# Order of the loads, shared Q/K buffers and new places for batches 1 to 3 in a fused window-attention and mixer kernel

## The chip, the core and the metric

The kernel runs on one core of one Trainium2 chip. The metric is the device time of a run in microseconds (us), given as the median of 11 runs. A core has five engines that each work through a queue of their own in order: TensorE (PE; its weight loads are shown apart as PEld), VectorE (DVE), ScalarE (ACT), GpSimd (POOL) and SyncE (SP). They wait for one another through semaphores. Transfers between HBM and SBUF are issued from a queue (here POOL's for loads with a change of type, SP's for stores and for transposes inside SBUF) and carried out by 16 DMA engines. Matmuls write to PSUM, of which VectorE and ScalarE copy the results out.

## The reference

```python
# attention, 8 batches, 8 heads, 576 rows, head size 64, window 64
scores = scale * np.matmul(q, k.transpose(0, 1, 3, 2))
mask = (rel >= 0) & (rel < window)            # rel = row - column
attn = exp(where(mask, scores, -1e9) - max) ; attn = attn / (sum + 1e-09)
x = (attn @ v), heads side by side            # [8, 576, 512]
# mixer
h = xt @ U @ V          # over the 576 rows, rank 32; xt is x transposed
u = x + h.transpose(0, 2, 1)
ch = np.maximum(u @ w_ch1, 0.0) @ w_ch2       # 512 -> 2048 -> 512
out = u + ch
```

Each row sees at most 64 columns, so only the diagonal and the next lower block of 64 by 64 are computed.

## The kernel before, in words

**Two streams woven together.** The mixer works on 9 chunks of 512 rows (all 8 x 576 = 4608 rows laid end to end). Chunk c has 32 slots: 16 pieces `ch1` (four matmuls of 512 columns each, then a ReLU out of PSUM on ScalarE or VectorE, by the table `DVE_RELU`), and 16 pieces `ch2` (four output tiles of 128 rows, four quarters each; after the fourth quarter VectorE adds u and SP stores the tile). Behind each slot stand pieces of the attention of batch b = c + 1, as the tables `PLACE`, `PLACE_1` and `PLACE_2` say: a piece's number is the slot behind which it is written. This written order is each engine's queue. There is no planner: the order is by hand. Batch 0's attention runs ahead of the chunks, with idle matmuls (`turn_over`, L718) in between.

**The pieces of a batch.** `T` brings Q and K into transposed form: for batches 0 and 1 from a grouped load (six rows per partition) by TensorE transposes (`tr`, L262) with a copy by ScalarE (K) and VectorE (Q), for the later ones by `TX`, ten DMA transposes from SP's queue (L285) into `kf` and `qf`, of which there is one each. `S` is the scores of two heads and their exponential (L326, L346), the last piece, `SC8`, those of the last block of all heads; `M` multiplies with the mask on VectorE. `PV` multiplies with V (L388) and normalises on VectorE with a reciprocal and a multiplication (L410, L411). V is kept twice: `vA` by tiles of 128 rows, and `vB` shifted by 64 rows, which is copied out of `vA` (`shift_v`, L149 and L152): on POOL for batches 0 and 1, on VectorE for the others, in slot 8 or 24. `U` is the low-rank product with its copy `hh` (L502), `V` its second half (`psv`, L566) with the addition to x (L579), and `UT` the transposed u that `ch1` reads: for batches 0 to 2 by TensorE (L598) through the single buffer `tp` and a ScalarE copy (L601), from batch 3 on (`NXU` = 3) by DMA transposes from SP's queue (L594).

**The loads.** POOL issues them in this order: Q and K of batch 0, V of batch 0, the first weights `w1b` (L217), Q and K of batch 1 in grouped form (L117), V of batch 1 (L135, L140), the second weights `w2b` in four parts (L225), then Q and K of batch 2, V of batch 2 and so on. Each DMA of POOL's queue waits for the one eight places before it to land: the first `w2b` load is the eighth after the second `w1b` load, and was issued as that landed.

Of the kernel before, what the change touches and what calls it, by code (L numbers as in the profile page):

```python
# [8 lines left out]
ACT = mybir.ActivationFunctionType  # L9
# [7 lines left out]
def kernel(  # L17
# [24 lines left out]
    NGR = 2  # L42
    NXB = 2
    NXU = 3
    GP = S // GR
    NFULL = S // P
    CH = 512
# [9 lines left out]
    outf = out.rearrange("b s m -> (b s) m")  # L57

    const = ctx.enter_context(tc.tile_pool(name="const", bufs=1))
    kg_pool = ctx.enter_context(tc.tile_pool(name="kg", bufs=4))  # L60
    uT_pool = ctx.enter_context(tc.tile_pool(name="uT", bufs=3))
    u_pool = ctx.enter_context(tc.tile_pool(name="un", bufs=14))
    c1_pool = ctx.enter_context(tc.tile_pool(name="c1", bufs=1))
# [24 lines left out]
    xs = [const.tile([P, NT, H, D], BF16, name=f"xs{i}") for i in range(2)]  # L88
    vA = [const.tile([P, NFULL, H, VW], BF16, name=f"vA{i}") for i in range(2)]
    vB = [const.tile([P, NFULL, H, VW], BF16, name=f"vB{i}") for i in range(2)]  # L90
    kn = [const.tile([P, NT, H, D], BF16, name=f"kn{i}") for i in range(2)]
    qn = [const.tile([P, NT, H, D], BF16, name=f"qn{i}") for i in range(2)]

    kf = const.tile([P, NT * HP * P], BF16, name="kf")
    qf = const.tile([P, NT * HP * P], BF16, name="qf")
    kt, qt = ([f[:, j * S : (j + 1) * S] for j in range(HP)] for f in (kf, qf))
    kx, qx = (f.rearrange("p (t j w) -> p t j w", t=NT, j=HP) for f in (kf, qf))
    pts = const.tile([P, HP, 2, NB - 1, W], BF16, name="pts")
    ptl = const.tile([P, HP, 2, W], BF16, name="ptl")

# [3 lines left out]
    def load_kq(b, split):  # L104
        grouped = b < NGR
        if grouped:
            kb = kg_pool.tile([GP, H, GR, D], BF16, name="kg")
            qb = kg_pool.tile([GP, H, GR, D], BF16, name="qg")
        else:
            kb, qb = kn[b % 2], qn[b % 2]  # L110
        loaded[b] = (kb, qb)
        if grouped:
            step = 4 if split else H
            for h0 in range(0, H, step):
                hs = slice(h0, h0 + step)
                for t, src in ((kb, k), (qb, q)):
                    nc.gpsimd.dma_start(  # L117
                        out=t[:, hs, :, :].rearrange("p h c d -> p h (c d)"),
                        in_=src[b, hs, :, :].rearrange("h (p c) d -> p h (c d)", c=GR),
                    )  # L120
                    yield
        else:
            for t in range(NT):
                rows = P if t < NFULL else W
                for dst, src in ((kb, k), (qb, q)):
                    nc.gpsimd.dma_start(  # L126
                        out=dst[0:rows, t, :, :],
                        in_=src[b, :, t * P : t * P + rows, :].rearrange("h p d -> p h d"),
                    )
                yield  # L130
# [15 lines left out]
    def shift_v(b, copy, tiles):  # L146
        va, vb = vA[b % 2], vB[b % 2]
        lo, hi = tiles.start, tiles.stop
        copy(out=vb[W:P, lo:hi, :, :], in_=va[W:P, lo:hi, :, :])  # L149
        last = min(hi, NFULL - 1)  # L150
        if lo < last:
            copy(out=vb[0:W, lo:last, :, :], in_=va[0:W, lo + 1 : last + 1, :, :])  # L152


    kq0 = load_kq(0, True)
# [35 lines left out]
    nc.vector.memset(xs[0][W:P, NT - 1, :, :], 0.0)  # L191
    nc.vector.memset(xs[1][0:W, 0, :, :], 0.0)
    for i in range(2):
        nc.vector.memset(kn[i][W:P, NFULL, :, :], 0.0)
        nc.vector.memset(qn[i][W:P, NFULL, :, :], 0.0)


    nc.sync.dma_start(
# [16 lines left out]
    w1v = moe_w_ch1.rearrange("(c p) n -> p c n", p=P)  # L215
    for lo, hi in ((0, 1024), (1024, 2048)):
        nc.gpsimd.dma_start(out=w1b[:, :, lo:hi], in_=w1v[:, :, lo:hi])  # L217
    for t in range(NFULL):
        shift_v(0, nc.gpsimd.tensor_copy, range(t, t + 1))
    for _ in load_kq(1, False):  # L220
        pass
    load_v(1)
    w2v = moe_w_ch2.rearrange("(i p) m -> p i m", p=P)
    for i in range(0, NFC, 4):
        nc.gpsimd.dma_start(out=w2b[:, i : i + 4, :], in_=w2v[:, i : i + 4, :])  # L225
    for t in range(NFULL):
        shift_v(1, nc.gpsimd.tensor_copy, range(t, t + 1))

    u_tiles = {}
    uT_tiles = {}  # L230
# [7 lines left out]
    def attention(b, spare=False):  # L238
# [4 lines left out]
        x = xs[odd]  # L243
        g0 = (b * S) // P
        pcs = {}

        grouped = b < NGR
        turn = [0]
# [26 lines left out]

        def TQ(j):
            def f():
                copy = nc.scalar.copy if spare and j == 3 else nc.vector.tensor_copy
                copy(out=place_of(qt, j), in_=tr(qb, j, b == 1))
            return f  # L280

        def TX(t):
# [306 lines left out]
        def UT(t):  # L589
            def f():  # L590
                g = g0 + t
                dst = uT_of(g // TPC)[:, g % TPC, :, :]
                if b >= NXU:
                    nc.sync.dma_start_transpose(out=dst, in_=u_tiles[g][:])  # L594
                    return
                tp = ps_tp.tile([P, NDC, P], BF16, name="tpu", tag="tp")
                for dc in range(NDC):
                    nc.tensor.transpose(  # L598
                        tp[:, dc, :], u_tiles[g][:, dc * P : (dc + 1) * P], ident[:]
                    )  # L600
                nc.scalar.copy(out=dst, in_=tp[:])  # L601
            return f
# [26 lines left out]
        return pcs  # L629


    DVE_RELU = {0: (8, 10, 11, 13, 15), 1: (2, 4, 6, 9, 10, 12, 13)}
    DVE_RELU_N = (0, 1, 2, 4, 5, 6, 8)

    def mlp(c):
        uTc = uT_of(c)
        c1 = [None] * NFC

        def ch1(i):
            def f():  # L640
                ps = psum["mm"].tile([P, CH], FP32, name="psA", tag="mm")
                for dc in range(NDC):
                    nc.tensor.matmul(  # L643
                        ps[:],
                        w1b[:, dc, i * P : (i + 1) * P],
                        uTc[:, :, dc, :],
                        start=(dc == 0),
                        stop=(dc == NDC - 1),
                    )
                c1[i] = c1_pool.tile([P, CH], BF16, name=f"c1_{i}")  # L650
                if i in DVE_RELU.get(c, DVE_RELU_N):
                    nc.vector.tensor_relu(out=c1[i][:], in_=ps[:])  # L652
                else:
                    nc.scalar.activation(out=c1[i][:], in_=ps[:], func=ACT.Relu)  # L654
            return f

        acc = {}
# [19 lines left out]
                    nc.sync.dma_start(out=outf[g * P : (g + 1) * P, :], in_=osb[:])  # L677
            return f

        return [ch1(i) for i in range(NFC)] + [ch2(t, r) for t in range(TPC) for r in range(4)]  # L680


    PLACE = {
# [7 lines left out]
    }  # L691
    PLACE_0 = {"V": [0, 0, 1, 2, 2, 3, 4, 4]}
    PLACE_1 = {
        "T": [11, 11, 12, 12, 13, 13, 14, 14],
        "S": [12, 13, 14, 15, 15],
        "M": [13, 14, 15, 16, 16],
        "PV": [17, 17, 18, 19, 20],
        "U": [22],
        "V": [23, 24, 25],
        "UT": [25, 26, 27, 28, 29],  # L700
        "TX": [20, 22, 24, 26, 28],
    }
    PLACE_2 = {
        "S": [8, 8, 11, 11, 13],
        "M": [9, 10, 12, 13, 14],
        "PV": [16, 16, 18, 18, 20],
        "TX": [13, 14, 15, 16, 17],
        "U": [21],
        "V": [23, 24, 25],
        "UT": [25, 26, 27, 28, 29],  # L710
    }


# [2 lines left out]
    def turn_over(n, cols=CH):  # L716
# [14 lines left out]
        op0=ALU.mult,  # L731
        op1=ALU.add,
    )
    pair = maskA[:, 0, 1:3, :].rearrange("p (o n) w -> p o (n w)", o=1)
    nc.vector.tensor_copy(
        out=maskA[:, 0, 3:7, :].rearrange("p (o n) w -> p o (n w)", o=2),
        in_=pair.to_broadcast([P, 2, 2 * W]),
    )
    nc.vector.tensor_copy(out=maskA[:, 0, 7, :], in_=maskA[:, 0, 1, :])
    nc.vector.tensor_scalar(  # L740
        out=maskB[:],
        in0=maskA[:, 0, :, :],
        scalar1=30000.0,
        scalar2=-30000.0,
        op0=ALU.mult,
        op1=ALU.add,
    )
    order = "K0 K1 B0 B1 Q0 Q1 S0 S1 K2 K3 B2 Q2 B3 Q3 S2 S3 B4 S4"
    for what in order.split():
        j = int(what[1])  # L750
        if what[0] in "SB":
            a[what[0]][j]()
        else:
            a["T"][2 * j + (what[0] == "Q")]()
        if what == "Q1":
            load_low_rank()
        turn_over({"B1": 1, "Q1": 1, "S1": 1, "Q3": 1}.get(what, 0))
    nc.vector.tensor_copy(out=maskA[:, 1, :, :], in_=maskA[:, 0, :, :])
    nc.scalar.copy(out=ub[0][:], in_=uf[0][:])
    nc.scalar.copy(out=vrep[:, W : W + S], in_=vf[:])  # L760
    for t in range(NT + 2):
        if t < NT:
# [5 lines left out]
            a["idle"](1)  # L768
    for f in [a["U"][NT - 1]] + a["X3"] + a["HT"]:
        f()  # L770
    first.close()
    psum["mm"] = ctx.enter_context(
        tc.tile_pool(name="ps_mm", bufs=3, space=bass.MemoryType.PSUM)
    )


    for c in range(NCH):
        slots = [[] for _ in range(NSLOT + 1)]

        def place(b, parts, where):  # L780
            if b not in att:
                att[b] = attention(b)
            for part in parts:
                for f, s in zip(att[b][part], where[part]):
                    slots[s].append(f)

        b = c + 1
        if b < B:
# [3 lines left out]
            if b + 1 < B:  # L792
                load_v(b + 1)
            if b + 2 < B:
                for _ in load_kq(b + 2, False):
                    pass
            where = {1: PLACE_1, 2: PLACE_2}.get(b, PLACE)
            if b < NXB:
                place(b, ("T",), where)
            if b == 1:  # L800
# [2 lines left out]
            for bs, slot in ((b, 8), (b + 1, 24)):  # L803
                if 1 < bs < B and (slot == 24) == (bs > 2):
                    slots[slot].append(
                        lambda bs=bs: shift_v(bs, nc.vector.tensor_copy, range(NFULL))
                    )
            place(b, ("S", "M", "PV"), where)
            if NXB <= b + 1 < B:
                place(b + 1, ("T",), {"T": where["TX"]})  # L810
# [35 lines left out]
```

The softmax here doesn't subtract the row's maximum and nothing guards it: scores larger than these inputs give would overflow.

## Time and profile before

| | us |
|---|---|
| median of 11 runs | 321.82 |
| lowest and highest of them | 320.56 and 324.8 |
| the profiled execution's own time | 321.33 |
| its span | 319.6 |
| first product of chunk 0 | 23.66 |
| first `ch2` of chunk 0 | 43.29 |
| first product of chunk 1 | 65.97 |
| first product of chunk 2 | 99.77 |
| first product of chunk 3 | 132.08 |
| last store issued | 316.63 |

How to read the lines: a row of groups gives line, engine, operation, the tiles it writes and reads, shapes and count, then busy time and the mean of one in ns, and the idle time ahead of it with what ended it. A row of the timeline gives start, length, engine, line, operation and tiles; matmuls overlap, so the next one starts before the length of the last has run out. A row of waits gives who waited for whom, the sum, the count and the longest. The granted clock is a share of TensorE's full speed.

### The profile page before, as it was taken

The page shows a single profiled execution, that of the slowest core. Times are in us where ns is not written, and L with a number is a line of the kernel's source. Part 1 is how long each engine was busy: PE and PEld are TensorE (multiplying, and loading weights), DVE is VectorE, ACT ScalarE, POOL GpSimd, SP SyncE. Part 2 cuts the span into 40 slices and gives each one's busy share as a digit, 9 for nine tenths or more (in the row PEclk, how much of TensorE's full clock was granted, in tenths as well). Part 3 has the DMA queues.
Part 4 walks back from the last instruction along what each step waited for, and adds up shares of the span by engine and source line. Part 5 has one row for each costly group of instructions (what it writes and reads, how often), then busy time and mean ns, then how long its engine had stood idle before and what let it go on. Part 6 is the DMA issues. An engine that isn't in the chain of part 4 may idle for free.

```text
span 319.6 us, 6811 instructions
## 1 busy us (share of the span) xinstructions
PE 306.4 (96%) x2829; PEld 149.8 (47%) x2855; DVE 162.8 (51%) x293; ACT 101.8 (32%) x160; POOL 103.2 (32%) x134
## 2 busy tenths in 40 slices
PE   7779988999999999999999999999999999999995
PEld 6544543544545544454445444544454444444442
DVE  4464584527775745475647464756374443016011
ACT  3545550336224450335024502450245003201500
POOL 8692696645734744554541400000000000000000
PEclk9999997999999999999999999999999999999999
DMA  7999999999999999999999982344200520020011
GB/s 105 161 223 202 156 200 171 120 167 191 143 138 210 161 139 149 184 193 157 138 210 177 144 158 100 68 100 95 105 2 2 115 99 2 9 89 33 2 66 66
DMA packets 151871, 39.56 MB, mean 124 GB/s; under 512 B 140960, under 2 KB 146080, under 8 KB 151840
## 3 DMA queue, kind: packets, MB, share of 16 engines
q0 software_dynamic: 100096, 18.36, 78.7%
q1 hardware_dynamic: 51744, 20.77, 35.8%
q8 instruction: 22, 0.36, 0.4%
q14 instruction: 9, 0.07, 0.1%
HBM read 37.14 MB, written 9.44 MB: 146 GB/s over the span
## 4 chain that ended last, share of the span: by engine, by line
PE 79%; DMA 13%; POOL 5%; issue 1%; SPq 1%; DVE 0%; POOLq 0%
PE psA L643 35%; PE psU L665 35%; DMA qg<-in_q_dram 5%; DMA vA<-in_v_dram 3%; DMA qn<-in_q_dram 2%; DMA uTc<-un 2%; PE psv L566 2%; PE sc L326 2%; PE xw L388 2%; POOL vB L149 1%; PE xr L388 1%; POOL vB L152 1%; PE pshh L487 1%; POOL vA L135 1%; PE tpu L598 1%
## 5 line engine op out<-in xcount | busy, mean ns | idle before, releaser
L665 PE MATMUL psU<-w2b,c 128*128 128x512 bf16 x555 | 131.5, 382 | 3.6 <-DMA w2b<-in_moe_w_ch_dram 2.2
L643 PE MATMUL psA<-uTc,w1b 128*128 128x512 bf16 x576 | 131.0, 380 | 0.5 <-DVE uTc L553 0.4
L665 PEld LDWEIGHTS <-c 128*128 128x128 bf16 x576 | 55.5, 98 | 67.2 <-issue 3.8
L643 PEld LDWEIGHTS <-w1b 128*128 128x128 bf16 x576 | 54.0, 98 | 65.1 <-issue 1.3
L654 ACT ACTIVATE c<-psA 128x512 bf16<-128x512 f32 x83 | 49.6, 597 | 91.2 <-PE psA L643 91.2
L674 DVE TENSOR_TENSOR osb<-psU,un 128x512 f32<-128x512 f32 x36 | 24.9, 691 | 84.3 <-PE psU L665 84.0
L652 DVE TENSOR_SCALAR c<-psA 128x512 bf16<-128x512 f32 x61 | 42.0, 689 | 24.7 <-PE psA L643 24.7
L579 DVE TENSOR_TENSOR un<-psv,xs 128x512 bf16<-128x512 f32 (+1 forms) x40 | 25.4, 684 | 22.1 <-PE psv L566 22.0
L135 POOL DMA_DIRECT2D vA<-in_v_dram x32 | 28.2, 888 | 22.6 <-DVE rce L444 7.8
L346 ACT ACTIVATE pts<-sc 128x1024 bf16<-128x1024 f32 x32 | 31.4, 1028 | 2.7 <-PE sc L326 2.6
L126 POOL DMA_DIRECT2D qn<-in_q_dram x30 | 25.7, 855 | 19.1 <-DMA qn<-in_q_dram 7.8
L126 POOL DMA_DIRECT2D kn<-in_k_dram x30 | 25.4, 848 | 18.8 <-DMA vA<-in_v_dram 9.5
L379 ACT ACTIVATE ptl<-low 128x256 bf16<-128x256 f32 x5 | 1.9, 384 | 64.8 <-PE high L326 64.8
L352 DVE TENSOR_TENSOR pts<-pts,maskA 128x1024 bf16<-128x1024 bf16 x28 | 19.2, 686 | 0.1
L326 PEld LDWEIGHTS <-kf 64*64 64x64 bf16 x704 | 10.0, 107 | 8.5 <-issue 8.3
L326 PE MATMUL sc<-qf,kf 64*64 64x128 bf16 (+1 forms) x624 | 12.2, 212 | 1.6 <-issue 0.8
L388 PEld LDWEIGHTS <-pts 128*64 128x64 bf16 x512 | 10.4, 112 | 6.8 <-issue 4.6
L566 PE MATMUL psv<-hh,vrep 128*128 128x512 bf16 x40 | 12.5, 379 | 0.0
L455 DVE TENSOR_TENSOR xs<-xw,rcw 128x896 bf16<-128x896 f32 x10 | 10.9, 1092 | 0.3
L411 DVE TENSOR_TENSOR xs<-xr,rcp 128x512 bf16<-128x512 f32 (+1 forms) x15 | 10.4, 691 | 0.5
L502 ACT CAST hh<-pshh 128x512 bf16<-128x512 f32 x7 | 4.1, 581 | 18.4 <-PE pshh L495 18.4
L601 ACT COPY uTc<-tpu 128x512 bf16<-128x512 bf16 x9 | 5.3, 586 | 11.2 <-PE tpu L598 11.2
(102 smaller groups left out, 160.2 us busy)
## 6 DMA issues: line engine op xcount, KB each, us to landing
out_dram<-osb SPq DMA_DIRECT2D x36, 256.0 KB, 2.4
vA<-in_v_dram POOLq DMA_DIRECT2D x32, 128.0 KB, 10.3
kn<-in_k_dram POOLq DMA_DIRECT2D x24, 128.0 KB, 12.3
qn<-in_q_dram POOLq DMA_DIRECT2D x24, 128.0 KB, 12.0
w1b<-in_moe_w_ch_dram POOLq DMA_DIRECT2D x2, 1024.0 KB, 15.8
w2b<-in_moe_w_ch_dram POOLq DMA_DIRECT2D x4, 512.0 KB, 13.1
kg<-in_k_dram POOLq DMA_DIRECT2D x2, 288.0 KB, 5.8
qg<-in_q_dram POOLq DMA_DIRECT2D x2, 288.0 KB, 6.8
```

What stands on the lines that cost most here:

```text
L126: nc.gpsimd.dma_start(out=dst[0:rows, t, :, :], in_=src[b, :, t * P : t * P + rows, :].rearrange("h p d -> p h d"),)
L135: nc.gpsimd.dma_start(out=va[:, t, :, 0:D], in_=v[b, :, t * P : (t + 1) * P, :].rearrange("h p d -> p h d"),)
L326: nc.tensor.matmul(sc[g][r0 : r0 + W, col * W : (col + n) * W], keys_of(j, u, rs), queries_of(j, blk, n, rs), start=not spare, stop=last o ...
L346: nc.scalar.activation(out=dst, in_=sc[:], func=ACT.Exp, scale=scale)
L352: nc.vector.tensor_tensor(out=dst, in0=dst, in1=maskA.rearrange("p g n w -> p g (n w)"), op=ALU.mult)
L388: nc.tensor.matmul(dst, pts[:, h // 2, h % 2, blk, :] if blk < NB - 1 else ptl[:, h // 2, h % 2, :], rhs, start=True, stop=True,)
L579: nc.vector.tensor_tensor(out=u_tiles[g][rs, :], in0=ps[0][rs, n, :], in1=x[rs, t, :, :].rearrange("p h d -> p (h d)"), op=ALU.add,)
L643: nc.tensor.matmul(ps[:], w1b[:, dc, i * P : (i + 1) * P], uTc[:, :, dc, :], start=(dc == 0), stop=(dc == NDC - 1),)
L652: nc.vector.tensor_relu(out=c1[i][:], in_=ps[:])
L654: nc.scalar.activation(out=c1[i][:], in_=ps[:], func=ACT.Relu)
L665: nc.tensor.matmul(acc[t][:], c1[i][:, t * P : (t + 1) * P], w2b[:, i, :], start=(i == 0), stop=(i == NFC - 1),)
L674: nc.vector.tensor_tensor(out=osb[:], in0=acc[t][:], in1=u_tiles[g][:], op=ALU.add)
```

## The change

- **Order of the loads.** The four `w2b` loads are issued ahead of the five loads of batch 1's V.
- **Copies of V.** For batch 0 five of the seven copies stay on POOL and two go to ScalarE. For batch 1 all seven leave POOL for VectorE, as pieces `SV` in slots 21 to 24, each written ahead of the `PV` of the same slot.
- **Buffers.** `kf` and `qf` exist twice, by the batch's parity. The grouped loads no longer have buffers of their own: they use the memory of `kn` and `qn`. So batch 3's Q and K loads are written behind slot 14 of chunk 0.
- **Places.** Batches 1, 2 and 3 have new tables. A number above 100 means the next chunk. Batch 1's PV goes from slots 17 to 20 to slots 21 to 24, and what follows it moves accordingly; batch 2's scores go from slots 8 to 13 to slots 14 to 18; batch 3 gets a table of its own.
- **Transposes of u.** Batch 3's go from SP's DMA to TensorE (`NXT` = 4), while the other choices that hung on `NXU` stay.
- **Mask.** The bias mask is made of three blocks and repeated on ScalarE with one block on VectorE; the multiplied mask is completed only after batch 0's attention.
- **Others.** The first two `ch1` pieces of chunk 0 are joined, with their matmuls in turn; the ReLU tables change; one more idle matmul; batch 0's fourth Q copy goes to VectorE.

```diff
+    kr = [const.tile([P, H * GR * D], BF16, name=f"kr{i}") for i in range(2)]
+    qr = [const.tile([P, H * GR * D], BF16, name=f"qr{i}") for i in range(2)]
+    kn, qn = (
+        [r[:, 0 : NT * DM].rearrange("p (t h d) -> p t h d", t=NT, h=H) for r in rs] for rs in (kr, qr)
+    )
+    kfs = [const.tile([P, NT * HP * P], BF16, name=f"kf{i}") for i in range(2)]
+    qfs = [const.tile([P, NT * HP * P], BF16, name=f"qf{i}") for i in range(2)]
...
+    def shift_high(b, copy, t):
+        copy(out=vB[b % 2][W:P, t, :, :], in_=vA[b % 2][W:P, t, :, :])
+
+    def shift_low(b, copy, t):
+        copy(out=vB[b % 2][0:W, t, :, :], in_=vA[b % 2][0:W, t + 1, :, :])
...
-    for t in range(NFULL):
-        shift_v(0, nc.gpsimd.tensor_copy, range(t, t + 1))
+    for t in range(2):
+        shift_high(0, nc.gpsimd.tensor_copy, t)
+        shift_low(0, nc.gpsimd.tensor_copy, t)
+    shift_low(0, nc.gpsimd.tensor_copy, 2)
     for _ in load_kq(1, False):
         pass
-    load_v(1)
     w2v = moe_w_ch2.rearrange("(i p) m -> p i m", p=P)
     for i in range(0, NFC, 4):
         nc.gpsimd.dma_start(out=w2b[:, i : i + 4, :], in_=w2v[:, i : i + 4, :])
-    for t in range(NFULL):
-        shift_v(1, nc.gpsimd.tensor_copy, range(t, t + 1))
+    load_v(1)
...
-                copy = nc.scalar.copy if spare and j == 3 else nc.vector.tensor_copy
-                copy(out=place_of(qt, j), in_=tr(qb, j, b == 1))
+                nc.vector.tensor_copy(out=place_of(qt, j), in_=tr(qb, j, b == 1))
...
-                if b >= NXU:
+                if b >= NXT:
                     nc.sync.dma_start_transpose(out=dst, in_=u_tiles[g][:])
...
-    DVE_RELU = {0: (8, 10, 11, 13, 15), 1: (2, 4, 6, 9, 10, 12, 13)}
+    DVE_RELU = {0: (7, 9, 11, 15), 1: (2, 4, 6, 8, 10, 12, 15), 2: (1, 3, 6, 7, 9, 10)}
...
+        ups = [ch1(i) for i in range(NFC)]
+        if c == 0:
+            ups[0:2] = [ch1(0, 1), lambda: None]
...
     PLACE_1 = {
-        "T": [11, 11, 12, 12, 13, 13, 14, 14],
-        "S": [12, 13, 14, 15, 15],
-        "M": [13, 14, 15, 16, 16],
-        "PV": [17, 17, 18, 19, 20],
-        "U": [22],
-        "V": [23, 24, 25],
-        "UT": [25, 26, 27, 28, 29],
-        "TX": [20, 22, 24, 26, 28],
+        "T": [10, 10, 11, 11, 12, 12, 13, 13],
+        "S": [11, 12, 13, 14, 15],
+        "M": [12, 13, 14, 15, 16],
+        "SV": [21, 22, 23, 24],
+        "PV": [21, 22, 23, 24, 24],
+        "U": [26],
+        "V": [27, 28, 28],
+        "UT": [29, 30, 31, 31, 102],
+        "TX": [27, 28, 29, 30, 31],
     }
     PLACE_2 = {
-        "S": [8, 8, 11, 11, 13],
-        "M": [9, 10, 12, 13, 14],
-        "PV": [16, 16, 18, 18, 20],
-        "TX": [13, 14, 15, 16, 17],
-        "U": [21],
-        "V": [23, 24, 25],
-        "UT": [25, 26, 27, 28, 29],
+        "S": [14, 14, 17, 17, 18],
+        "M": [15, 16, 18, 19, 19],
+        "PV": [20, 20, 22, 22, 24],
+        "TX": [20, 21, 22, 23, 24],
+        "U": [26],
+        "V": [27, 28, 29],
+        "UT": [29, 30, 31, 102],
+    }
+    PLACE_3 = {
+        "S": [5, 5, 5, 8, 8],
+        "M": [5, 6, 7, 9, 10],
+        "PV": [12],
+        "TX": [12, 13, 14, 15, 16],
+        "U": [18],
+        "V": [20, 21, 22],
+        "UT": [22, 23, 24, 25, 102],
     }
...
+    repeat(nc.scalar.copy, maskB)
...
-        turn_over({"B1": 1, "Q1": 1, "S1": 1, "Q3": 1}.get(what, 0))
-    nc.vector.tensor_copy(out=maskA[:, 1, :, :], in_=maskA[:, 0, :, :])
+        turn_over({"B1": 1, "Q1": 1, "S1": 1, "B2": 1, "Q3": 1}.get(what, 0))
     nc.scalar.copy(out=ub[0][:], in_=uf[0][:])
+    for t in range(2, NFULL):
+        shift_high(0, nc.scalar.copy, t)
...
+                if b < NGR:
+                    slots[14].append(load_next)
+                else:
+                    load_next()
...
+            if b == 1:
+
+                def land(t):
+                    def f():
+                        shift_high(1, nc.vector.tensor_copy, t)
+                        if t > 0:
+                            shift_low(1, nc.vector.tensor_copy, t - 1)
+                    return f
+
+                att[1]["SV"] = [land(t) for t in range(NFULL)]
+                place(b, ("SV",), where)
             place(b, ("S", "M", "PV"), where)
```

## The prediction

> **What bounds the kernel now.** I read the page's busy row first, then the stretches in 40 us pieces, then TensorE's waits, and only then the pieces around them.
>
> ```profile
> PE 306.4 (96%) x2829; PEld 149.8 (47%) x2855; DVE 162.8 (51%) x293; ACT 101.8 (32%) x160; POOL 103.2 (32%) x134
> ```
> ```profile
> 160.00:200.00 40.00, 39.84 (x385) 19.00 (x386) 22.11 (x38) 12.57 (x20) 8.21 (x10) 1.00 1.37 157
> ```
> ```profile
> PE psU L665 <- DMA w2b<-in_moe_w_ch_dram: 2.2, 3, 1.1
> ```
>
> TensorE is the bound: 39.84 of 40 us busy in a stretch of the steady part. Only its holes can be won, and each new hole is lost in full, since TensorE runs its queue in order. After 24 us the one large hole is the wait for the second weights, 2.2 us in the row and 0.2 us more at 50.23 (put down there to a batch-2 load that landed in the same moment): 2.4 us. Behind it the clock falls:
>
> ```profile
> 46.28:49.69 3.41, 1.55 (x21) 0.81 (x21) 2.39 (x5) 0.00 (x0) 1.26 (x2) 1.00 2.10 168
> 49.69:53.10 3.41, 3.19 (x23) 1.25 (x22) 1.51 (x3) 0.00 (x0) 2.72 (x4) 0.50 2.43 155
> ```
>
> The columns are stretch, length, busy of PE, PEld, DVE, ACT, POOL, granted clock, DMA share, GB/s. TensorE was busy 1.55 of 3.41 us with no hole over 1.15 us, and the next 3.41 us ran at 0.50: 1.7 us lost. Together 4.1 us is all that this stage has to give.
>
> **What the early weights remove.** In POOL's queue the four w2b loads trade places with batch 1's five V loads. The last V load was issued at 23.66 and took 16.1 us, so V held the queue from qg's landing (19.23 + 15.4 = 34.6) to 39.8; the last w2b load, issued at 35.65, landed 13.8 us later, at 49.5. Without V ahead it lands near 49.5 - 4.3 = 45.2 (five V loads took 0.9 to 1.3 us each there). The product needs its last quarter at 43.29 + 3 x 0.863 = 45.9 (a slot is four matmuls of 0.216 us: 36 in 7.77 us in the chain). The wait goes: -2.4, and its clock dip: -1.7. V then lands from about 46 to 49, its first reader stands at 48.5: just in time, taken as nothing; each us that it is late costs one.
>
> Batch 1's transposes move from slot 11 to 10, which ends at 34.2 + 0.3; qg lands at 34.6: +0.25.
>
> **Batch 1's PV (slots 21 to 24).** The seven V copies leave POOL for VectorE, and each pair stands in VectorE's queue behind the normalisation of the PV before it, while the next PV needs it. How long the queue holds is read at the last PV of batch 1:
>
> ```profile
> 53.78 1.90 PE L665 MATMUL psU<-w2b,c 128*128 128x512 bf16 x8
> ```
> ```profile
> 53.91 0.21 DVE L410 RECIPROCAL rcp<-xr 128x8 f32<-128x8 f32 x1 [1.03 <-PE xr L388]
> 54.16 0.69 DVE L411 TENSOR_TENSOR xs<-xr,rcp 128x512 bf16<-128x512 f32 x1
> ```
> ```profile
> L149 DVE COPY vB<-vA x6: 699/699/1076, 72.9 to 222.4; 64x2080 bf16<-64x2080 bf16 x6
> ```
> ```profile
> L152 DVE COPY vB<-vA x6: 557/559/636, 73.7 to 223.1; 64x1560 bf16<-64x1560 bf16 x6
> ```
>
> TensorE is free of PV at 53.78, VectorE is done with it at 54.85: 1.07 us. A copy of 64x520 isn't in VectorE's trace; 2080 elements take 0.70 and 1560 take 0.56, so 0.14 + 520 x 0.00027 = 0.28 us (bounds: 0.18 by pure proportion, 0.62 by POOL's own row). Two are 0.5 with their overlap, and 0.1 passes until TensorE sees the semaphore: 1.67 us against one slot of 0.863, so TensorE stands 0.8 us. This happens ahead of the second, third and fourth PV; in slot 23 the result's addition (0.69, of which about 0.63 after overlap) is queued between them, so 1.44 there. 0.8 + 1.44 + 0.8 = +3.05 (2.4 to 4.5 by the bounds). Queued behind each waiting matmul is all of the product.
>
> **Three psv in slots 27, 28, 28.** The third needs the PSUM buffer of the first, which VectorE frees after the result's addition and two additions of 0.64: 0.1 + 0.7 + 1.28 + 0.1 = 2.2 us after the first began; TensorE gets there after 0.43 + 0.86 + 0.43 = 1.7: +0.5 (0 to 0.8).
>
> **Transposes of u in the last slot.** One pass through the single tp buffer:
>
> ```profile
> 59.68 0.39 PE L598 MATMUL tpu<-ident,un 128*128 128x128 bf16 x4
> ...
> 60.76 0.39 PE L598 MATMUL tpu<-ident,un 128*128 128x128 bf16 x4
> ```
> ```profile
> 60.10 0.59 ACT L601 COPY uTc<-tpu 128x512 bf16<-128x512 bf16 x1 [3.40 <-PE tpu L598]
> ```
>
> From the transposes' start to the end of ScalarE's copy 1.01 us, with the semaphore 1.09; 0.22 of it is TensorE's own work and a slot covers the rest. Now two stand in slot 31 of chunk 0, followed at once by chunk 1's first product, which reads that tile: 2 x 0.87 = +1.74. Chunk 1 ends the same way with one: +0.87. These are the surest terms (1.8 to 2.8 in sum).
>
> **Chunk 1, batch 2.** Its scores move from slots 8 to 13 to slots 14 to 18, the last two masks to slot 19 behind the result's addition, and PV starts in slot 20. Two exponentials of 1.0 us after slot 17, then addition and mask 0.69 each, leave the last mask at 4.3 us after slot 17's product, where PV wants it at 3.9: +0.4. In slot 24 batch 3's V copies (0.70 + 0.60) now come ahead of the last PV's normalisation, and batch 2's `U` product in slot 26 waits for that: normalised at about 7.6, wanted at 6.9 after PV's start: +0.7 (both together 0 to 2).
>
> **Batch 3's Q/K transposes.** The second kf/qf takes away their wait for batch 2's scores, but in SP's queue they now stand after chunk 1's first store, in slots 20 to 24 instead of 13 to 17.
>
> ```profile
> 77.67 1.19 SPq L285 DMA_TRANSPOSE kf<-kn  x1
> ...
> 92.56 1.42 SPq L285 DMA_TRANSPOSE qf<-qn  x1
> ```
> ```profile
> 100.73 0.21 PE L326 MATMUL low<-qf,kf 64*64 64x64 bf16 x1
> ```
>
> From first issue to last landing (7.3 us after 92.56) 22.2 us, 0.8 us ahead of their first reader. After the change the store is ready 20.7 us into chunk 1 (20 slots 17.3, scores 1.7, transpose 0.2, addition and store 1.5), so they land at 42.9; batch 3's scores, whose first piece reads the last tile, now stand in slot 5 of chunk 2: 33.8 (chunk 1 before, 65.97 to 99.77) + 2.0 (waits above) + 5.4 = 41.2. So +1.7; beside fewer loads the ten transposes take 15 us (the late ones, 201.18 to 216.2), then 0; with 23.5 (those from 104.68 to 128.2) 3. I take 1.5. No POOL queue is delayed by it before the next loads, which have 20 us of room.
>
> **Work added on TensorE.** Batch 3's five u tiles leave SP's queue for TensorE: 5 x 0.22 = +1.1. It gives nothing back: the DMA form cost no visible wait (TensorE 19.90 of 20 us busy from 120 to 140). One more idle matmul in the start: +0.1.
>
> **Edits costed at nothing.** The mask's repeat on ScalarE lies under the load that first Q and K wait for (ScalarE idle 4.65 us there); if it were late, 0.4. The fourth Q copy on VectorE instead of ScalarE, and two V copies of batch 0 on ScalarE, are done by 14.1 and 18.3, wanted at 14.9 and 19.0. The joined first two products wait for the same VectorE copy as before. The new ReLU split moves work between two engines that are half idle. Sharing kr/qr makes batch 3's loads wait for transposes that end 20 us before POOL reaches them. The next kf/qf lets later transposes start early, where nothing waits.
>
> **Sum.** -2.4 - 1.7 + 0.25 + 3.05 + 0.5 + 1.74 + 0.87 + 0.4 + 0.7 + 1.1 + 0.1 = +4.6, with the late transposes +6.1. The profiled execution took 321.33 (span 319.6, 1.7 around it), 0.5 below the median of 321.82; the sum is put on the median: 327.9, rounded to 328.0.
>
> **The clock.** The Trainium skill (TensorE: Matmul & The Clock Gate, "Why this matters for your kernels") asks only for no idle gap over about 3 us. By that rule none of the new holes (1.5 us at most) costs clock, and neither could the old ones have; the row above shows half clock after holes of 0.8 and 1.15. The measurement decides. A stretch of 3.41 us that is 45% busy was followed by half clock, one with 2.19 busy (15.55 to 18.97) wasn't; the new PV stage comes to 40 to 60%, by where the stretch begins, chunk 0's end to 50%. By the rule the sum is 328.0, by the row up to 1.7 more for each of three places. I leave it in the range: one dip is about as likely as none.
>
> **The rivals.** (1) All waits form but the transposes come in time: 326.5; for it speaks 15 us late in the trace, against it that the loads are still running at 100 us. (2) Two or three dips on top of late transposes: 331.5 to 333; the old dip speaks for it, the clock at 1.00 from 12 to 22 us with several holes speaks against it. (3) Faster: the hand-overs from VectorE and ScalarE to TensorE cost nothing, because TensorE reaches slots 22 to 24 and 31 later than I place it or the producers are earlier. They are 3.05 + 0.5 + 1.74 + 0.87 + 0.4 + 0.7 = 7.3 of the sum; with all gone and the transposes in time, 321.8 + 4.6 - 7.3 = 319.2. It decides below 2.7 us for all of them. Against it: each distance is read from a row, and in-order queues leave no way around. (4) Half of them: 322.8, no change that can be told.
>
> **How the numbers follow.** Main case 0.50 (328.0; its own range 325.5 to 330.5, one dip in it), rival 1 0.18, rival 2 0.12, rival 3 0.08, rival 4 0.12, half of which reaches past +0.5%. 0.5% is 1.6 us, about what eleven runs from 320.56 to 324.8 can tell. Faster 0.08, same 0.06, slower 0.86. The range 323.0 to 331.5 leaves out rival 3, the low part of rival 4 and most of rival 2.
>
> **What would show it.** Right: no wait for w2b; psU at full clock at 50 us; waits of xr for vB copies on VectorE; two holes of 0.87 at chunk 0's end, one at chunk 1's; the first score of batch 3 waiting for qf; batch 3's tpu on TensorE. Wrong: w2b landing after 46 (the gain shrinks), V after 49 (it turns into its wait), PV without a hole, or the steady part from chunk 3 on moved at all: there I expect the same 32.1 us a chunk.

## The result and the profile after

The changed kernel takes 327.71 us (median of 12 runs, 326.36 to 331.21), the kernel before beside it 321.39 (47 runs, 319.25 to 324.92): a ratio of 1.0202, 95% interval 1.0177 to 1.0228. It is slower by about 2%, clear of the noise. The profiled execution took 327.91 us, its span is 326.2.

The busy row of its page:

```profile
PE 308.5 (95%) x2850; PEld 151.3 (46%) x2876; DVE 165.2 (51%) x300; ACT 106.4 (33%) x169; POOL 97.5 (30%) x125
```

TensorE is busy 2.1 us longer, 1.1 of it in the five new transposes of u; the span is 6.6 us longer. So most of the loss is holes. Where it arises is read from the first product of each chunk. The last two columns belong to experiments told below.

| length in us | before | after | e5 | e12 |
|---|---|---|---|---|
| up to chunk 0 | 23.66 | 24.12 | 23.68 | 23.97 |
| chunk 0 | 42.31 | 45.47 | 40.62 | 38.19 |
| chunk 1 | 33.80 | 35.35 | 35.44 | 33.80 |
| chunk 2 | 32.31 | 33.20 | 33.20 | 33.55 |
| chunk 3 | 32.10 | 32.32 | 32.32 | 32.32 |

From chunk 4 on both kernels need the same 32.09 us a chunk: in the 40 us that begin 4.1 us ahead of chunk 4, as the stretch shown of before did, TensorE is again busy for 39.84. TensorE's waits in the changed kernel (who waits for whom, sum, times, longest):

```profile
PE xr L397 <- DVE vB L159: 3.1, 3, 1.6
PE psA L653 <- ACT uTc L610: 1.3, 2, 0.7
PE unread L742 <- DVE idle L163: 1.3, 1, 1.3
PE psA L653 <- DVE maskA L773: 1.1, 1, 1.1
...
PE tpu L607 <- ACT uTc L610: 0.7, 1, 0.7
...
PE psv L575 <- DVE un L588: 0.5, 1, 0.5
```

The wait for the second weights is gone: their last quarter landed at 45.0, and the product runs through. In its place stand batch 1's PV (`xr` for the shifted V), the transposes of u (`uTc`) and `psv`. The wait for `maskA` stands at the first product of chunk 0, and was 0.4 before. It isn't the mask's: the first half of `w1b`, issued at 9.45, landed 14.6 us later here, just ahead of the product's start at 24.12, and 13.6 later before. In the experiments e3 and e11 a hole of nearly the same length at the same matmul is put down to this load, in e4 to e8 it is 0.44 again. It is the spread of a load from run to run, 0.7 us in this execution.

VectorE around the second and third PV (start, length, operation, idle before):

```profile
49.84 0.69 DVE L420 TENSOR_TENSOR xs<-xr,rcp 64x512 bf16<-64x512 f32 x1
50.46 0.64 DVE L156 COPY vB<-vA 64x520 bf16<-64x520 bf16 x1
51.11 0.29 DVE L159 COPY vB<-vA 64x520 bf16<-64x520 bf16 x1
51.94 0.21 DVE L419 RECIPROCAL rcp<-xr 128x8 f32<-128x8 f32 x1 [0.54 <-PE xr L397]
52.19 0.69 DVE L420 TENSOR_TENSOR xs<-xr,rcp 128x512 bf16<-128x512 f32 x1
52.88 0.69 DVE L685 TENSOR_TENSOR osb<-psU,un 128x512 f32<-128x512 f32 x1
53.60 0.65 DVE L156 COPY vB<-vA 64x520 bf16<-64x520 bf16 x1
54.26 0.29 DVE L159 COPY vB<-vA 64x520 bf16<-64x520 bf16 x1
```

And TensorE's first matmuls behind them:

```profile
51.45 0.19 PE L397 MATMUL xr<-vB,pts 128*64 128x65 bf16 x1 [0.77 <-DVE vB L159]
...
52.77 0.22 PE L397 MATMUL xr<-vA,pts 128*64 128x65 bf16 x1
54.60 0.19 PE L397 MATMUL xr<-vB,pts 128*64 128x65 bf16 x1 [1.61 <-DVE vB L159]
...
56.84 0.21 PE L397 MATMUL xr<-vB,pts 128*64 128x65 bf16 x1 [0.70 <-DVE vB L159]
```

Each pair of copies ends 0.05 us before PV goes on, and begins only when the normalisation, and once the result's addition, is done. A hole costs more than its wait says, since the matmul ahead of it runs out with nothing beside it: from the last matmul on `vA` to the first on `vB` 0.99, 1.83 (52.77 to 54.60) and 0.92 us pass, where 0.03 would without a wait. PV's holes cost 3.65 us, not 3.1. In the stretches around it the clock falls, as it did before at the weights (columns as there):

```profile
52.90:56.30 3.40, 1.63 (x21) 0.72 (x20) 2.77 (x6) 0.00 (x0) 2.90 (x4) 1.00 2.20 189
56.30:59.70 3.40, 2.53 (x35) 1.64 (x36) 2.18 (x6) 0.00 (x0) 3.40 (x6) 0.50 2.19 157
```

At the end of chunk 0:

```profile
68.54 0.38 PE L607 MATMUL tpu<-ident,un 128*128 128x128 bf16 x4 [0.67 <-ACT uTc L610]
69.59 2.10 PE L653 MATMUL psA<-uTc,w1b 128*128 128x512 bf16 x9 [0.67 <-ACT uTc L610]
```

Two hand-overs with a wait of 0.67, and a third at 104.94. From start to start it is 1.05 us, 0.22 of it TensorE's own work, so each costs 0.83. Batch 3's Q/K transposes were issued from 90.30 on. The last of them and its first reader:

```profile
103.93 1.22 SPq L294 DMA_TRANSPOSE qf<-qr  x1
```
```profile
110.43 0.21 PE L335 MATMUL low<-qf,kf 64*64 64x64 bf16 x1
```

It landed 5.9 us after its issue, at 109.8, which is 19.5 us after the first was issued. The reader waited for nothing.

### The profile page after: what moved, and what is told of

It reads as the page before. It is cut to its first block, busy times and chain, and to the rows that moved or that the text cites. A ratio compares the mean times of both kernels' runs of the same rounds, so it can differ in the third digit from the quotient of the medians.

```text
span 326.2 us, 6873 instructions
## 1 busy us (share of the span) xinstructions
PE 308.5 (95%) x2850; PEld 151.3 (46%) x2876; DVE 165.2 (51%) x300; ACT 106.4 (33%) x169; POOL 97.5 (30%) x125
## 4 chain that ended last, share of the span: by engine, by line
PE 89%; DVE 6%; DMA 2%; ACT 1%; issue 1%; DVEq 0%; POOLq 0%
PE psA L653 39%; PE psU L676 36%; PE sc L335 3%; PE psv L575 2%; PE xw L397 2%; PE xr L397 2%; DMA kr<-in_k_dram 2%; DVE xs L420 1%; DVE osb L685 1%; PE tpu L607 1%; PE tpg L272 1%; PE sc L325 1%; PE pshh L496 1%; ACT pts L355 1%; ACT uTc L610 1%
## 5 line engine op out<-in xcount | busy, mean ns | idle before, releaser
L665 ACT ACTIVATE c<-psA 128x512 bf16<-128x512 f32 x85 | 50.6, 597 | 92.8 <-PE psA L653 92.8
L663 DVE TENSOR_SCALAR c<-psA 128x512 bf16<-128x512 f32 x59 | 40.7, 690 | 31.2 <-PE psA L653 31.2
L127 POOL DMA_DIRECT2D kr<-in_k_dram x30 | 25.9, 862 | 11.9 <-DMA kf<-kr 3.5
L127 POOL DMA_DIRECT2D qr<-in_q_dram x30 | 26.4, 880 | 8.4 <-DMA qf<-qr 4.7
L610 ACT COPY uTc<-tpu 128x512 bf16<-128x512 bf16 x14 | 8.2, 586 | 16.2 <-PE tpu L607 16.2
```

The source lines that it names most:

```text
L127: nc.gpsimd.dma_start(out=dst[0:rows, t, :, :], in_=src[b, :, t * P : t * P + rows, :].rearrange("h p d -> p h d"),)
L663: nc.vector.tensor_relu(out=c1[i][:], in_=ps[i][:])
L665: nc.scalar.activation(out=c1[i][:], in_=ps[i][:], func=ACT.Relu)
```

## The experiments

The theory was that the loss is a sum: the weights give 4.1 back, PV's copies take 3.05 and a clock dip, the hand-overs 3, the transposes of u 1.1, the late Q/K transposes 1.5. Each part was then undone alone. Chunk times below are from each run's trace.

**e1: the early weights taken back.** The changed kernel with one line moved.

```diff
+    load_v(1)
     w2v = moe_w_ch2.rearrange("(i p) m -> p i m", p=P)
...
-    load_v(1)
```

> The changed kernel with one part undone: batch 1's V is loaded ahead of the second weights again, all else as changed. If the order of the loads is worth what the prediction says, the last w2b load lands near 49.5 us again, TensorE waits for w2b some 2 us in slots 17 to 19 of chunk 0, the three waits for V's copies (3.1 us in sum) stay, and the half-speed stretch stays or comes twice: 329.5 to 332 us. If the order only moves one wait to another place, the time stays at 327.7 us.

329.97 us; ratio to before 1.0251 (1.0214 to 1.0289), where the changed kernel has 1.0202 (1.0177 to 1.0228). Among TensorE's waits:

```profile
PE xr L397 <- DVE vB L159: 2.1, 2, 1.3
PE psU L676 <- DMA w2b<-in_moe_w_ch_dram: 1.5, 1, 1.5
```

The weights' wait is back with 1.5 us, and PV has two holes in place of three, so chunk 0 is only 0.54 us longer (46.01 against 45.47). The other 1.8 us of this execution stand ahead of chunk 0, which starts at 25.90 instead of 24.12. There, two stretches ran at half clock (columns as before):

```profile
12.97:16.38 3.41, 2.04 (x67) 1.48 (x68) 1.08 (x2) 1.66 (x2) 1.22 (x2) 0.99 2.06 139
16.38:19.79 3.41, 2.35 (x52) 1.99 (x52) 2.18 (x6) 2.75 (x6) 2.14 (x5) 0.50 1.21 231
19.79:23.18 3.39, 3.39 (x33) 1.70 (x32) 2.08 (x5) 0.25 (x1) 3.39 (x5) 0.50 1.24 215
```

By the ratios the early weights are worth about 1.6 us within the change, with intervals that overlap, and by the trace less; in neither the whole 4.1.

**e2: nothing but the early weights**, on the kernel before.

```diff
-    load_v(1)
     w2v = moe_w_ch2.rearrange("(i p) m -> p i m", p=P)
...
+    load_v(1)
```

> The kernel before with one part alone: the second weights loaded ahead of batch 1's V, its copies still on POOL and all places as before. My theory: the wait for w2b (2.4 us) goes, but V lands from 46 to 50 us while its PV stands in slots 17 to 20 (45 to 50 us) behind POOL's copies, so TensorE waits about 2.4 us there instead, and batch 2's loads are issued behind those copies, some 9 us later than before: about as before, 320 to 323.5 us. Rival: the early weights alone give their whole 4.1 us: 317.3 us.

329.85 us, ratio 1.0225 (1.0164 to 1.0286): both expectations missed. Chunk 0 takes 38.96 us, 3.35 less than before, so the part does what it says. But POOL's copies of V now stand in its queue until the later V load has landed (the first starts at 45.85 instead of 36.39), and the loads of batches 2 and 3 are issued behind them: batch 2's first at 51.22 instead of 41.38. The delay comes back in TensorE's waits:

```profile
PE tpu L598 <- DVE un L579: 3.1, 1, 3.1
PE sc L326 <- DMA qf<-qn: 2.6, 1, 2.6
PE psA L643 <- DMA uTc<-un: 2.2, 1, 2.2
```

Chunks 1 to 3 lose 7.8, 2.1 and 0.9 us. So the copies had to leave POOL once V is loaded later. Another 2.0 us stand ahead of chunk 0, where this execution ran at half clock from 16.2 to 23.1 us, as e1's did. The order of the loads isn't what does that, since e1 has the other one.

**e3: the copies ahead of the normalisation**, still on VectorE.

```diff
-        "SV": [21, 22, 23, 24],
+        "SV": [20, 21, 21, 21],
```

> The changed kernel with batch 1's V copies written earlier in VectorE's queue (slots 20, 21, 21, 21 instead of 21 to 24), so that they no longer stand behind the normalisation of the PV before; nothing else is moved. If the place in VectorE's queue is the cause, the three waits shrink from 3.1 to under 0.6 us (-2.5), and if the half-speed stretch hangs on these holes it goes too (-1.7): 323.5 us, or 325.2 if the clock falls anyway. If V's landing is the cause, nothing changes: 327.7 us.

327.62 us, ratio 1.0172 (1.0105 to 1.0239): the time of the rival, V's landing, but not its waits. The PV holes shrink from 3.1 to 1.0, the half clock behind them is gone, and chunk 2 starts 3.7 us earlier (101.21 against 104.94). Nothing of it is left at the end, because of a wait that the changed kernel doesn't have:

```profile
PE low L335 <- DMA qf<-qr: 2.3, 1, 2.3
```

**e4: the copies on ScalarE.**

```diff
-                        shift_high(1, nc.vector.tensor_copy, t)
+                        shift_high(1, nc.scalar.copy, t)
...
-                            shift_low(1, nc.vector.tensor_copy, t - 1)
+                            shift_low(1, nc.scalar.copy, t - 1)
```

> The changed kernel with batch 1's seven V copies on ScalarE instead of VectorE, in the same slots. ScalarE has nothing else between 45 and 60 us, so the copies (about 0.6 us each) run as V lands, from 46 to about 51 us. My theory: the three waits of 3.1 us nearly vanish, and so does the half-speed stretch: 323 us, 324.7 if the clock falls anyway. Rival: ScalarE's longer copies become the wait (4.2 us of them against three slots): 326 to 327.7 us.

327.44 us, ratio 1.0172 (1.0121 to 1.0224): again a time in the rival's range, but ScalarE's copies are not waited for. No PV hole is left. Chunk 0 is 40.62 instead of 45.47, so the holes (3.65) and the clock behind them (the other 1.2) cost 4.85 us together. Chunk 2 starts at 99.89, as before the change, and then:

```profile
PE low L335 <- DMA qf<-qr: 2.9, 1, 2.9
```

```profile
104.40:107.80 3.40, 1.05 (x5) 0.29 (x3) 0.05 (x1) 1.19 (x2) 1.53 (x2) 0.99 2.22 114
107.80:111.20 3.40, 2.80 (x56) 1.71 (x57) 0.43 (x1) 2.33 (x4) 1.78 (x3) 0.51 1.44 242
```

The wait and the half clock behind it make chunk 2 4.28 us longer than in the changed kernel (37.48 against 33.20), nearly all of what chunk 0 saved. SP's queue tells why (issue, length):

```profile
84.53 0.33 SPq L688 DMA_DIRECT2D out_dram<-osb  x1
85.03 1.24 SPq L294 DMA_TRANSPOSE kf<-kr  x1
```

The transposes follow the chunk's first store and start 5.3 us earlier than in the changed kernel; the last lands at 108.3, 1.5 us earlier. In e3 (issued 86.4, landed 109.0), e4 and the changed kernel they take 22.6, 23.2 and 19.5 us. So in all three they land between 108 and 110, however long TensorE is held up ahead of them: a floor under chunk 2.

**e5 and e13: the floor taken away, with and without the PV holes.** e5 is e4 with this line, e13 the changed kernel with nothing but this line:

```diff
-        "TX": [20, 21, 22, 23, 24],
+        "TX": [13, 14, 15, 16, 17],
```

> The kernel with the V copies on ScalarE, and beside it batch 3's ten DMA transposes written in slots 13 to 17 of chunk 1 instead of 20 to 24, so that they no longer stand behind chunk 1's first store in SP's queue. If that place is the cause of the wait for qf (2.95 us there), they start near 76 us instead of 85, land near 100, the wait goes, and the half-speed stretch behind it with it: 322.8 us, 324.5 if the clock falls somewhere all the same. If the DMA engines are the bound whatever the order, the last tile still lands near 108 and the time stays at 327.4.

> The changed kernel with nothing but batch 3's ten DMA transposes written behind slots 13 to 17 of chunk 1 again, ahead of that chunk's first store, instead of slots 20 to 24; the copies of batch 1's V stay on VectorE. Theory: the late transposes are a floor under chunk 2 that the holes of chunk 0 hide, so taking the floor away alone gives nothing: 327 to 328 (ratio 1.015 to 1.02), no wait for qf, the PV holes of 3 us and the half clock behind them as in the changed kernel. Together with e4 (copies alone, 327.44) and e5 (both, 322.74) this is the fourth cell. Rival, the prediction's sum: the late transposes are a term of their own, worth 1.5 here: 326.2. Second rival: the transposes are all of e5's gain and the copies nothing: 323.

e5: 322.74 us (20 runs), ratio 1.0042 (1.0022 to 1.0062). e13: 327.36 us, ratio 1.0177 (1.0144 to 1.021). The four cells are

| | transposes behind the store | ahead of it |
|---|---|---|
| copies on VectorE | 327.71 | 327.36 |
| copies on ScalarE | 327.44 | 322.74 |

Either alone gives nothing that can be told from zero, both together 5.0 us. The two costs lie side by side, and only the longer of the two counts: without the PV holes the reader comes earlier and waits for the transposes. e13's waits for `vB` are those of the changed kernel:

```profile
PE xr L397 <- DVE vB L159: 3.2, 3, 1.6
PE psA L653 <- ACT uTc L610: 1.3, 2, 0.7
```

**e6: batch 3's u by DMA again.**

```diff
-    NXT = 4
+    NXT = 3
```

> The changed kernel with one part undone: batch 3's five transposes of u go through SP's DMA again instead of TensorE. By the prediction they cost TensorE 5 x 0.22 = 1.1 us for nothing: 326.6 us. Rival: in the shifted order they land after chunk 3 begins, and the wait eats the gain: 327.7 us or more.

331.84 us, ratio 1.0311 (1.026 to 1.0362), where 326.6 was expected. TensorE saves its 1.1 us and waits at chunk 3's start:

```profile
PE psA L653 <- DMA uTc<-un: 2.7, 1, 2.7
```

With the new places of batch 3 the transposed u by DMA is late. The 1.1 us are the price of not waiting for it. This execution, at 329.46, is the fastest of the six. The others' mean clocks, 0.979 to 0.994, point to as many as four stretches at half clock, and how much of the 4.1 us by which the median is longer comes from there is open.

**e7: the holes kept, the clock held up.** Idle matmuls of 240 columns (5, 12 and 5) stand ahead of the second, third and fourth PV of batch 1.

```diff
+                for _ in range({1: 5, 2: 12, 3: 5}.get(t, 0) if b == 1 else 0):
+                    nc.tensor.matmul(
+                        xr[:, 0, 264:504], idle[:, 0:P], idle[:, 0:240], start=True, stop=True
+                    )
```

> The changed kernel with idle matmuls (5, 12 and 5 of 240 columns, 0.1 us each) put ahead of the three PV pieces that wait, into PSUM columns that nothing reads; they fill about two thirds of the holes and leave the waits as they are. If half clock follows a low busy share, the stretch near 56 us is gone and the time falls by up to 1.7: 326 to 326.5 us. If it follows from something else, it stays and so does the time: 327.7.

327.3 us, ratio 1.0164 (1.012 to 1.0208), above the 326 to 326.5 expected. The stretches around PV:

```profile
51.30:54.70 3.40, 2.97 (x33) 1.99 (x33) 2.74 (x7) 0.00 (x0) 3.40 (x5) 1.00 2.30 169
54.70:58.10 3.40, 2.93 (x45) 1.86 (x45) 2.76 (x7) 0.00 (x0) 3.40 (x5) 1.00 2.14 188
```

The dip is gone and chunk 0 takes 44.22 instead of 45.47, 1.25 us less: what e4 had left for the clock. The mean clock of its six runs is 0.998 to 1.000, that of the changed kernel's twelve 0.984 to 0.995, where one stretch at half clock is worth 0.5 x 3.41 / 326 = 0.005: each of the twelve lost at least about one stretch to half clock, and none of the six did. The gain ends at the floor again, with 1.1 us of waiting for `qf` and a chunk 2 that is 1.2 us longer.

**e8, e10, e11, e12: what the change could give.** e8 is e5 with PV and all behind it one slot earlier, so that no transposes of u stand in the last slots:

```diff
-        "SV": [21, 22, 23, 24],
-        "PV": [21, 22, 23, 24, 24],
-        "U": [26],
-        "V": [27, 28, 28],
-        "UT": [29, 30, 31, 31, 102],
+        "SV": [19, 20, 20, 20],
+        "PV": [20, 21, 22, 23, 23],
+        "U": [25],
+        "V": [26, 27, 28],
+        "UT": [27, 28, 29, 30, 102],
...
-        "M": [15, 16, 18, 19, 19],
-        "PV": [20, 20, 22, 22, 24],
+        "M": [15, 16, 18, 18, 19],
+        "PV": [20, 20, 22, 22, 23],
...
-        "U": [26],
-        "V": [27, 28, 29],
-        "UT": [29, 30, 31, 102],
+        "U": [25],
+        "V": [26, 27, 28],
+        "UT": [28, 29, 30, 102],
```

> The kernel with copies on ScalarE and the transposes ahead, and beside it batch 1's and 2's PV, U, V and UT pieces one slot earlier, one UT in a slot and none in the last, so that no ScalarE copy stands between two chunks. By the prediction's terms the wait for the third psv (0.5), the two at chunk 0's end (1.34 measured) and the one at chunk 1's (0.67) go: 2.5 us less than the kernel with the transposes ahead, 320.3 us, or 322 with one half-speed stretch left. Rival: V lands too late for the earlier PV, which then waits what the rest gains: 322.8 us.

321.87 us (20 runs), ratio 0.9999 (0.9974 to 1.0024). The hand-overs and the `psv` hole are gone (chunk 1 starts at 61.69, chunk 2 at 97.63), and the next floor shows, batch 2's transposes, which stand behind chunk 0's first store:

```profile
PE sc L335 <- DMA qf<-qr: 1.9, 1, 1.9
```

e10 moves those ahead of it, e11 is e10 with `NXT` = 3:

```diff
-        "TX": [27, 28, 29, 30, 31],
+        "TX": [20, 20, 21, 21, 22],
```

> The kernel with the earlier u pieces, and beside it batch 2's ten DMA transposes written in slots 20 to 22 of chunk 0 instead of 27 to 31, ahead of two stores in SP's queue. They then start as batch 2's Q and K land, from 51 us instead of 57.5, and the wait of batch 2's scores for qf (1.94 us there) goes, with the half-speed stretch that follows it in most runs: 319.5 us, faster than the kernel before by 0.5 to 0.8%. Rival: the transposes slow batch 2's V and batch 3's loads by as much, and another wait for a transfer takes its place: 321.9 us.

> The same, with batch 3's five transposes of u through SP's DMA. If SP's queue and the DMA engines are free early enough now, TensorE has 1.1 us less to do: 318.4 us. If they land after chunk 3 begins, as in the changed kernel with this one part undone (2.65 us there), it is slower: 320 to 321.5 us.

Both missed: 326.85 us (ratio 1.0176, 1.0135 to 1.0217) and 330.47 (1.027, 1.022 to 1.0321). e10's longest wait, and VectorE's queue at its end, in the slowest of its six executions (329.7):

```profile
PE psv L575 <- DVE un L588: 8.2, 1, 8.2
```

```profile
98.74 0.70 DVE L150 COPY vB<-vA 64x2080 bf16<-64x2080 bf16 x1 [9.52 <-DMA vA<-in_v_dram]
99.47 0.81 DVE L153 COPY vB<-vA 64x1560 bf16<-64x1560 bf16 x1
100.21 1.26 DVE L588 TENSOR_TENSOR un<-psv,xs 128x512 bf16<-128x512 f32 x2
```

TensorE waits for an addition, the addition stands behind the copies of batch 3's V in slot 24, and these wait 9.5 us for their load. The four parts that they read landed at 92.0 to 98.5, in e8 at 80.9 to 88.8. The moved transposes run beside POOL's loads from 50.6 us on: the V load issued at 53.65 took 11.6 us (e8: 52.61, 6.4), and since each DMA of POOL's queue waits for the one eight places before it, batch 3's V was issued from 79.2 instead of 67.4. In e11 the same wait is 4.7, and 4.2 us ahead of chunk 3 come on top. The list of waits puts these to "issue"; the tile's own view names the transposes of u by DMA. e12 moves only those copies, to slot 8 of chunk 2, still four slots ahead of their reader:

```diff
-                if 1 < bs < B and (slot == 24) == (bs > 2):
+                if 1 < bs < B and (slot == 24) == (bs > 3):
```

> As e10, with VectorE's two copies of batch 3's V moved from slot 24 of chunk 1 to slot 8 of chunk 2, four slots ahead of batch 3's PV. Theory: the 8.15 us hole at batch 2's first psv in e10 was VectorE's queue standing behind these copies, which waited for batch 3's V load; with them moved, and no half clock of 1.7 to 3.4 us behind the hole, 326.85 - 8.15 - 1.0 = 317.7 (316.8 to 319), the lowest of all, with no wait for qf in chunk 1 and no wait of over 1 us in chunk 2. Rival: the load is what is late and another reader takes the wait: V itself, wanted at about 105, or batch 3's kf and qf, behind the same transfers; then 319.5 to 322, with one wait of 1.5 us or more and half clock behind it, and e8's time stays the floor.

319.27 us (9 runs, 318.94 to 321.56), ratio 0.9937 (0.9909 to 0.9965): 0.6% faster than the kernel before, and 0.3 us above the range expected. Its longest waits:

```profile
PE unread L742 <- DVE idle L163: 1.3, 1, 1.3
PE sc L335 <- issue: 1.0, 2, 0.7
PE tpg L272 <- DMA kr<-in_k_dram: 0.6, 1, 0.6
PE xr L397 <- DVE rcp L419: 0.6, 1, 0.6
```

All four lie ahead of chunk 0's first product or under 0.8 us each. Chunk 0 takes 38.19, 4.12 less than before: the 4.1 us of the early weights, nearly in full (0.2 is a transpose of u that now stands in chunk 1). Chunk 1 is as before, and chunks 2 and 3 pay 1.5, of which 1.3 are six transposes of u, five new and one moved on.

## Why the prediction came out

The forecast, 328.0, was 0.3 us off. That it was so close is luck: two errors of the sum cancelled.

| term | predicted | measured |
|---|---|---|
| wait for w2b, and its dip | -2.4, -1.7 | gone; e12's chunk 0 is 4.1 shorter, 0.2 of it a moved transpose |
| batch 1's transposes after qg, idle matmul | +0.25, +0.1 | 0.1 together (start to first `ch2` 19.71 against 19.63; e4 to e8 start as before) |
| PV behind the V copies | +3.05 | 3.65 |
| third psv | +0.5 | 0.51 of waiting |
| u in slot 31 and at the chunk ends | 1.74 + 0.87 | 1.66 + 0.83 |
| last mask, and V copies ahead of `U` | 0.4 + 0.7 | 0.21 of waiting + 0.25 (97.38 to 97.85, otherwise 0.22) |
| five u tiles on TensorE | +1.1 | 0.89 + 0.22 in chunks 2 and 3 |
| late Q/K transposes of batch 3 | +1.5 | 0 |
| a dip, in the range and not in the sum | 0 (1.7) | 1.2 |
| load of w1b | none | 0.7 in the profiled execution, by chance |

The measured column comes to 6.3 us, the spans differ by 6.6; 0.3 is not accounted for.

**Right for the reasons given:** the weights' gain (by e12; within the change e1 shows less of it), the places of PV's holes, `psv`, the doubled hand-over in slot 31 and the price of the u tiles on TensorE.

**Mis-sized:** PV, 3.65 instead of 3.05. The pair of copies takes 0.93 us (50.46 to 51.40) where 0.5 was taken from "0.14 + 520 x 0.00027". This is right for a copy that nothing holds up (0.29); but the other of each pair started in the middle of a DMA issue of POOL's and ended only behind it, after 0.45 to 0.65 (see the last section). VectorE gave part of it back: it finished the normalisation 0.85 us after TensorE left PV (52.88 against psU's start at 52.03), where 1.07 was taken. The mask and batch 3's V copies were 0.46 us instead of 1.1.

**Wrong:** "I take 1.5" for batch 3's transposes. The issue was placed well (20.7 us into chunk 1, as measured). What failed is the step "land at 42.9" against a reader at 41.2: they took 19.5 us where 22.2 had been read off, and landed 40.2 in, 0.6 ahead of the reader. More important, the sum treated it as a term to be added. e4, e5 and e13 show that it is the other branch of a maximum: what holds TensorE up in chunks 0 and 1 also moves the reader. With the PV holes gone the wait is 2.9 us, with them it is nothing. The total came out by luck: the dip (1.2), left out of the sum, took the place of the late transposes (1.5), and PV's 0.6 that of the mask and the V copies.

**Wrong as well:** that the DMA form of u gives nothing back. It was read from the trace of before, where nothing waits; in the new places e6 waits 2.7 us for it and is 4.1 us slower. This step did not change the total, since the change doesn't use the DMA form.

**The clock.** The prediction had set the rule of the Trainium skill (TensorE: Matmul & The Clock Gate, "Why this matters for your kernels", no idle gap over about 3 us) against a row of the trace. The runs stand with the row: the longest hole in the stretch ahead of the dip is 1.61 us, the stretch is 48% busy (1.63 of 3.40), and filling it to 2.97 takes the dip away (e7). But no share of busy time comes out as a threshold. The start of e1, 2.04 of 3.41 busy with no hole over 0.84, was followed by half clock; the end of chunk 0 in the changed kernel was not, and neither was the stretch with 2.19 that the prediction names:

```profile
66.54:69.95 3.41, 2.06 (x19) 1.19 (x17) 0.69 (x1) 1.76 (x3) 3.38 (x5) 1.00 2.62 119
```

What parts them is open. The same page's section "A second HAM failure mode: psum-queue depth-cycling" says that frequent short idling between groups of matmuls, there from cycling through PSUM banks, makes the clock go up and down too. It gives no figure; that short holes are enough fits what is seen here. "About as likely as none" was too low for the PV stage, which matched the old stretch in its busy time (1.55 before, 1.63 after, 1.64 in e1).

**The rivals.** That the hand-overs cost nothing (319.2) fell with every wait in the profile. That the transposes come in time (326.5) is what happened, with a dip of 1.2 on top: nearer to the measured course than the main case. Two or three dips stayed rare: of the twelve runs one, at 331.21 with a mean clock of 0.984, shows about three, and one, at 328.18 with 0.990, about two. The argument against them, full clock from 12 to 22 us, holds for some executions only: e1 and e2 ran at half clock there.

## What to carry to other kernels

Costs that hold up the same engine may be added; a transfer with its own clock is a floor, and stands in a maximum with everything ahead of its reader. So before a hole is mended, the slack of every transfer that is read after it has to be known: here 4.85 us mended alone were worth 0.3 (e4), and 4.6 with the floor moved (from e13 to e5). And before a piece is written into a shared in-order queue, look at what it waits for: copies that had done no harm in slot 24 cost 7.6 us once their load came late (e10), and moving them half a chunk on made the change a gain (e12).

## What the hardware showed unexpectedly

- The copy of 64 x 520 elements takes VectorE either 0.28 to 0.29 us or 0.35 to 0.72, whichever half of the partitions it writes: in the changed kernel L156 is the long one, in e3 mostly L159. What parts them is where the copy starts within a DMA issue of POOL's. In e3:

```profile
49.28 0.29 DVE L156 COPY vB<-vA 64x520 bf16<-64x520 bf16 x1
49.59 0.61 DVE L159 COPY vB<-vA 64x520 bf16<-64x520 bf16 x1
```
```profile
49.23 0.87 POOL L127 DMA_DIRECT2D qr<-in_q_dram  x1 [0.38 <-issue]
```

  The first starts 0.05 us into the issue and isn't held up; the second starts 0.36 into it and ends 0.10 after its end. So it is for the single copies of the six kernels that have them on VectorE beside POOL's issues (the changed one, e1, e3, e6, e7, e13): every long one started at least 0.26 us into an issue and ended 0.08 to 0.15 after its end, every short one started less than 0.2 into one, or in none. No run without POOL's issues was made.
- Ten DMA transposes take 15 us where POOL loads nothing (before, from 201.18 on) and 19.5 (after) to 23.2 (e4) beside loads. Issuing them 5.3 us earlier brought their end forward by 1.5.
- The loads are slowed as well: beside the transposes a V load took 11.6 us instead of 6.4 (e10, e8).
